# Landmark means of a Nyström attention: sums on GpSimd from q and k as they lie, in place of products on a second copy by rows

## The chip, the cores and the metric

The kernel runs on one core of a Trainium2 chip. The metric is the time of one execution on the device in microseconds; the median of the runs is what is compared. TensorE multiplies matrices, VectorE and ScalarE do elementwise work and reductions, GpSimd does elementwise work and issues the software transfers (loads), SyncE issues the stores.

## What is computed

Nyström attention over 8 batches and 8 heads, and then a feed-forward layer with a squared ReLU. The landmarks, on which the change works, are the means of 18 consecutive rows of q and of k (576 rows make 32 landmarks).

```python
q_lm = q.reshape(B, H, m, S // m, D).mean(axis=3)    # B = H = 8, S = 576, D = 64, m = 32
k_lm = k.reshape(B, H, m, S // m, D).mean(axis=3)
A = sm(q, k_lm); Bm = sm(q_lm, k_lm); C = sm(q_lm, k) # softmax of scaled products
Z = Bm.T / (norm1(Bm) * norminf(Bm) + 1e-06)          # norms over the last two axes
for _ in range(6):
    Z = 2 * Z - Z @ Bm @ Z
x = A @ Z @ C @ v                                     # then heads side by side: 4608 x 512
out = relu(x @ w_in) ** 2 @ w_out                     # 512 -> 2048 -> 512
```

All inputs and the output are fp32 in HBM.

## The kernel before

**Tiles.** A load turns q and k of one batch into bf16 in the tile X (lines 292 and 420): a partition holds one of four heads' 32 landmarks, so its row is the 18 x 64 elements that belong to one landmark; t = 0 is q and 1 is k, r is the half of the heads. Three X tiles take turns (batch b uses X of b mod 3), likewise V. A landmark is therefore a sum along a partition's own row, over 18 pieces of 64 elements.

**Landmarks.** Batches 0 to 2 sum on TensorE with an identity matrix as weights (`landmarks`, line 492). Batches 3 to 7 (`ROWS`, line 1187) load q and k a second time, by rows, into the tile XS (`load_xs`, line 427), and TensorE sums there with a 0/1 matrix `seg` as weights (`landmarks_rows`, line 477; 24 products of 256 columns a batch, line 485). VectorE or ScalarE copies the sums from PSUM with the scale 1/(8 x 18) to the bf16 tile LM (operation `lme`, lines 413 and 417); VectorE transposes them to LT (`lmt`, line 538).

**What follows on them.** From LT come the small matrix B (`B`, line 554), its softmax on VectorE and ScalarE (lines 560 to 570), the inverse by six steps, each a block-diagonal product `bd` on VectorE or GpSimd (line 630), two products on TensorE (`N`, line 693) and an update on VectorE (`U`, line 707), and the score products with q and k (`SS`, lines 724 and 729). The softmax of A takes VectorE through At, Amx, Asb, Asu and Aml (lines 1003 to 1020), that of C through Cmx (line 767) and ScalarE's Cex (line 770). The operations called `bt` (also line 630) and `BBT` begin the inverse.

**Feed-forward.** The attention is folded into the weights (`W`, line 886, copied to WP), so that the first layer is `F` (line 1050, 512 products), the ReLU `R` (line 1071 on ScalarE, 1073 on VectorE), the square `Q` (line 1078 on ScalarE, 1080 on VectorE and GpSimd) into the ring G, and the second layer `O` (line 1097, 592 products), whose result goes out through OS. The attention of a batch runs beside the feed-forward of the batches before it.

**Order.** Every operation has a name and the text ORDER (line 1204) lists them all in one sequence, with the PSUM bank (`@0`) and the engine if it isn't the first choice (`/A`, `/D`, `/P`). Each engine works through its own operations in this sequence. `Plan.schedule` (line 98) reckons with costs and due times to place filler products: `Plan.fillers` (line 160) puts products on a tile of ones (line 1171) into TensorE's gaps before the first operation O. An argument `port` marks operations of VectorE and GpSimd that the plan doesn't let overlap. GpSimd's queue holds the loads too, so a load stands behind what is ahead of it there.

Of the kernel before, what the change touches and what calls it, by code (L numbers as in the profile page):

```python
# [7 lines left out]
P = 128  # L8
# [8 lines left out]
H = 8  # L17
S = 576
D = 64
# [35 lines left out]
class Plan:  # L55
# [5 lines left out]
    BLOCK, FETCH, FETCH_LOADED, PROLOG = 256, 3.8, 6.2, 94  # L61
# [36 lines left out]
    def schedule(self, order):  # L98
# [4 lines left out]
        owner, landed, self.history, self.order = [None] * 8, [], [], []  # L103
        for word in order:
# [55 lines left out]
    def fillers(self, until, width, emit):  # L160
# [42 lines left out]
RATE = {"sw": 0.375e6, "hw": 0.2e6, "first": 0.375e6, "then": 0.405e6, "late": 0.29e6}  # L203
T0 = {"PE": 1.1, "ACT": 1.1, "DVE": 1.1, "POOL": 1.31, "SP": 1.1}
# [59 lines left out]
def kernel(  # L264
# [32 lines left out]
    XS = mk("XS", [96, 2, H, 6, D], BF16)  # L297
# [129 lines left out]
    def load_xs(b):  # L427
        for t in range(2):
            src = (q, k)[t][b].rearrange("h (p j) d -> p h (j d)", j=6)
            op(f"lx{b}.{t}", {"POOL": 0.57}, lambda e, t=t, src=src: nc.gpsimd.dma_start(  # L430
                XS[:, t].rearrange("p h j d -> p h (j d)"), src),
               W=[("XS", t)], nbytes=1179648, queue="sw")

# [25 lines left out]
    def attention(b):  # L459
# [17 lines left out]
        def landmarks_rows():  # L477
            pl_ = Bank(1, "att")
            view = lambda: bank(pl_)[:, 0:256].rearrange("p (t r d) -> p t r d", t=2, d=D)

            def lmx(e):
                xs = XS[:].rearrange("p t (r c) j d -> p t r c j d", r=2)
                for j in range(6):
                    for c in range(4):
                        nc.tensor.matmul(view()[quad(c)], lhsT=seg[:], rhs=xs[:, :, :, c, j, :],  # L485
                                         start=(j == 0), stop=(j == 5))
# [43 lines left out]
        for rs in rss:  # L530
            if b in ROWS:
                landmarks_rows()
# [600 lines left out]
    def loads(what, b):  # L1133
# [9 lines left out]
        elif what == "xs":  # L1143
            load_xs(b)
# [9 lines left out]
    for b in range(B):  # L1154
        if b in ROWS:
            loads("xs", b)
# [48 lines left out]
c0 ldk0.1 c1 ldq0.1 c13 c17 Bce0@0 ldq0.0 ldk0.0 ldq1.0 ldk1.0 c2 c14 c12 c3 lm0.1@6 ldk1.1 c5  # L1205
ldq1.1 c15 c6 c11 lmc0.10 lmc0.11 ldv0.10 ldv0.00 win10 ldv0.11 T0.11 c8 T0.01 lme0.1 lmt0.1
SC0.1@2 T0.00 T0.10 Cmx0.1 T1.00 c9 lm0.0@4 lme0.0 lmt0.0 B0@4 bk0 Bmx0 Cex0.1 CT0.1 Bsb0 Bex0
SC0.0@6 Cmx0.0 Bsu0 Brc0 win11 win01 Bml0/P SA0.1@2 Amx0.1b SA0.0@1 Amx0.0b c10 Cex0.0 Crc0 Bmb0/A
Btr0 Bcs0 Bnm0 Brn0 Amx0.0a Amx0.1a Asb0.0b Aex0.0b BBT0@4 Yi0 Asb0.1a Asb0.0a Asb0.1b Cmk0 win00
win21 Zi0/P win20 Aex0.1a lm1.0@0 lme1.0 Aex0.0a Aex0.1b N0.0@4 U0.0 N0.1@5 Asu0.0b lmt1.0 B1@0  # L1210
# [126 lines left out]
```

## Time and profile before

| | before |
|---|---|
| median of three runs, us | 264.32 |
| lowest and highest, us | 263.7 and 264.74 |
| profiled execution, us | 264.69 |
| its span, first to last instruction, us | 263.0 |
| its mean granted TensorE clock | 0.992 |

The page gives each engine's busy time over the span, then a chain of work followed back from the last instruction: shares of it tell which engine's work set the end. A row of a group reads: line, engine, operation, output and inputs, shape, count, then busy time in us, mean ns of one, and the idle time of the engine just before, with what ended it. A row of a window reads: the stretch, its length, the busy time of each engine with its instructions, the granted TensorE clock, the share of the transfer engines' time, and GB/s. A row in order of time has its start and its length in us. Line numbers are those of the kernel before.

### The profile page before, as it was taken

What the parts mean: (1) busy time and instruction counts of PE and PEld (TensorE: products, weight loads), DVE (VectorE), ACT (ScalarE), POOL (GpSimd) and SP (SyncE); (2) the same over time, 40 slices, a digit from 0 to 9 for tenths busy, and PEclk for the clock granted to TensorE, in tenths of its full rate; (3) what the DMA queues carried; (4) which work ended last, traced back from release to release, by engine and by line L of the source; (5) the groups of instructions that cost most, each with busy time, mean ns of one, the idle gap of its engine ahead of it and who ended that gap; (6) DMA issues with size and microseconds to landing.
All of it is one profiled execution on the core that took longest, in us unless ns stands there. A gap on an engine that the chain in (4) does not pass through costs nothing.

```text
span 263.0 us, 7571 instructions
## 1 busy us (share of the span) xinstructions
PE 253.5 (96%) x3098; PEld 141.0 (54%) x3098; DVE 208.8 (79%) x537; ACT 184.8 (70%) x334; POOL 75.5 (29%) x127
## 2 busy tenths in 40 slices
PE   7898999999999999999999999999999999999993
PEld 3465566466454656465545455466454655466542
DVE  2799698887999789997998999988898975657110
ACT  1552698489886799979687469797595896588211
POOL 8458675904303430140315520221010120000000
PEclk9999799999999999999999999999999999999999
DMA  6999999995997399848496399337301214053025
GB/s 105 204 185 205 209 207 205 193 208 113 196 223 151 63 205 212 204 87 176 64 231 107 46 190 227 70 60 139 96 2 40 38 31 101 2 120 81 2 61 140
DMA packets 25123, 34.18 MB, mean 130 GB/s; under 512 B 2432, under 2 KB 14464, under 8 KB 25088
## 3 DMA queue, kind: packets, MB, share of 16 engines
q0 software_dynamic: 19168, 24.25, 56.4%
q1 hardware_dynamic: 5760, 9.31, 13.1%
q8 instruction: 24, 0.39, 0.6%
q10 hardware_dynamic: 160, 0.13, 0.2%
q14 instruction: 11, 0.09, 0.1%
HBM read 48.50 MB, written 9.44 MB: 220 GB/s over the span
## 4 chain that ended last, share of the span: by engine, by line
PE 73%; DVE 15%; ACT 7%; issue 2%; POOL 2%; POOLq 0%; DVEq 0%; ACTq 0%
PE ps L1097 40%; PE ps L1050 19%; ACT RS L1071 3%; PE ps L886 3%; PE ps L815 2%; PE ps L1171 1%; DVE sm L767 1%; PE ps L729 1%; POOL X L424 1%; PE ps L485 1%; DVE G L1080 1%; ACT G L1078 1%; DVE RS L1073 1%; DVE TT L469 1%; DVE WP L415 1%
## 5 line engine op out<-in xcount | busy, mean ns | idle before, releaser
L1097 PE MATMUL ps<-w_out,G 128*128 128x512 bf16 (+1 forms) x592 | 139.1, 374 | 0.0
L1097 PEld LDWEIGHTS <-G 128*128 128x128 bf16 x592 | 54.5, 98 | 53.2 <-issue 5.5
L1050 PE MATMUL ps<-AT,WP 128*128 128x288 bf16 (+2 forms) x512 | 75.3, 286 | 0.9 <-ACT RS L1071 0.4
L1071 ACT ACTIVATE RS<-ps 128x576 bf16<-128x576 f32 (+2 forms) x99 | 62.1, 648 | 11.3 <-PE ps L1050 7.3
L1050 PEld LDWEIGHTS <-WP 128*128 128x128 bf16 x512 | 48.1, 98 | 21.9 <-issue 2.6
L1078 ACT ACTIVATE G<-RS 128x576 bf16<-128x576 bf16 (+2 forms) x80 | 53.6, 688 | 3.3 <-DVE RS L1073 2.4
L411 ACT COPY OS<-ps 128x512 f32<-128x512 f32 (+1 forms) x27 | 15.3, 568 | 18.8 <-PE ps L1097 16.2
L1073 DVE TENSOR_SCALAR RS<-ps 128x576 bf16<-128x576 f32 (+2 forms) x29 | 21.9, 757 | 7.2 <-PE ps L1050 3.5
L630 POOL TENSOR_TENSOR BD<-ST,blkb 128x256 bf16<-128x256 bf16 x15 | 10.5, 700 | 58.7 <-DVE ST L707 53.3
L411 ACT CAST WP<-ps 128x1024 bf16<-128x1024 f32 (+1 forms) x24 | 22.2, 962 | 7.2 <-PE ps L886 7.1
L469 DVE STREAM_TRANSPOSE TT<-X 128x576 uint32<-128x576 uint32 x32 | 24.0, 758 | 0.1
L1080 DVE TENSOR_TENSOR G<-RS 128x576 bf16<-128x576 bf16 (+1 forms) x40 | 18.1, 457 | 5.8 <-ACT RS L1071 5.5
L770 ACT ACTIVATE C<-ps,sm 128x576 bf16<-128x576 f32 x16 | 14.3, 906 | 11.8 <-DVE sm L767 11.8
L707 DVE SCALAR_TENSOR_TENSOR ST<-ST,ps 128x128 bf16<-128x128 bf16 (+1 forms) x48 | 12.8, 266 | 8.0 <-PE ps L693 4.7
L1171 PE MATMUL ps<-onesb 128*128 128x512 bf16 (+1 forms) x42 | 13.1, 404 | 1.5 <-DVE onesb L347 1.5
L440 POOL DMA_DIRECT2D V<-in_v_dram x24 | 13.2, 552 | 3.2 <-DMA XS<-in_k_dram 1.5
L415 DVE CAST WP<-ps 128x1024 bf16<-128x1024 f32 (+1 forms) x10 | 11.7, 1165 | 1.0 <-PE ps L886 0.9
L767 DVE TENSOR_REDUCE sm<-ps 128x1 f32<-128x576 f32 x16 | 11.6, 746 | 0.7 <-PE ps L729 0.5
L415 DVE COPY OS<-ps 128x512 f32<-128x512 f32 x10 | 6.7, 678 | 6.0 <-PE ps L1097 6.0
L630 POOL TENSOR_TENSOR BD<-Bt,blkb 128x256 bf16<-128x256 bf16 x4 | 2.7, 665 | 30.5 <-PE ps L693 17.1
L886 PE MATMUL ps<-w_in,ZC 64*32 64x512 bf16 x256 | 11.2, 397 | 0.1
L1080 POOL TENSOR_TENSOR G<-RS 128x512 bf16<-128x512 bf16 (+1 forms) x8 | 8.9, 1120 | 6.0 <-ACT RS L1071 6.0
(143 smaller groups left out, 304.3 us busy)
## 6 DMA issues: line engine op xcount, KB each, us to landing
out_dram<-OS SPq DMA_DIRECT2D x70, 128.0 KB, 2.5
X<-in_k_dram POOLq DMA_DIRECT2D x16, 288.0 KB, 9.0
X<-in_q_dram POOLq DMA_DIRECT2D x16, 288.0 KB, 7.8
XS<-in_q_dram POOLq DMA_DIRECT2D x5, 576.0 KB, 8.8
XS<-in_k_dram POOLq DMA_DIRECT2D x5, 576.0 KB, 9.9
V<-in_v_dram POOLq DMA_DIRECT2D x8, 288.0 KB, 6.1
w_in<-in_moe_w_in_dram POOLq DMA_DIRECT2D x8, 256.0 KB, 9.9
w_out<-in_moe_w_out_dram POOLq DMA_DIRECT2D x4, 512.0 KB, 9.8
```

The source lines that it names most:

```text
L411: nc.scalar.copy(o, i)
L415: eng(e).tensor_copy(o, i)
L469: op(f"T{b}.{t}{r}", {"DVE": v_(576)}, lambda e, r=r: nc.vector.transpose(tt[:, t, r].rearrange("p s m e -> p (s m e)").bitcast(U32), x[:, ...
L770: op(f"Cex{b}.{r}", {"ACT": a_(576) + 0.27}, lambda e, r=r: nc.scalar.activation(Cs[r][:].rearrange("p x u -> p u x"), cbanks(r), AF.Exp, ...
L886: nc.tensor.matmul(ps[quad(pos_a(c, r)), pW.at + r, :], lhsT=zcs[r][half, pos_c(c, r), :], rhs=w_in[half, c, 512 * ch:512 * ch + 512], sta ...
L1050: nc.tensor.matmul(ps[:, ph.at + i, 0:w], lhsT=wp[:, r, 128 * ff:128 * ff + 128], rhs=at[:, r, t0:t0 + w], start=(r == 0), stop=(r == 1))
L1071: nc.scalar.activation(rs, pair(ph, w), AF.Relu)
L1073: nc.vector.tensor_scalar(out=rs, in0=pair(ph, w), scalar1=0.0, scalar2=None, op0=ALU.max)
L1078: nc.scalar.activation(g, rs, AF.Square)
L1080: eng(e).tensor_tensor(g, rs, rs, ALU.mult)
L1097: nc.tensor.matmul(bank(po)[:, 0:c1 - c0], lhsT=G[:, f, lo:lo + P], rhs=w_out[:, f, c0:c1], start=(f == 0), stop=(f == NF - 1))
L1171: nc.tensor.matmul(ps[:, j, 0:w], lhsT=onesb[:, 0:P], rhs=x[:, 0:w], start=True, stop=True)
```

## The change

For batches 3 to 7 the tile XS, its loads and the products on it are taken out. GpSimd adds from X itself, in fp32, into the new tile SU: for each of q and k and each half of the heads the first nine pieces of 64 plus the last nine (`la`), and then for both halves together 4 + 4, 2 + 2, 1 + 1 and the ninth piece (`lb`). `lme` copies from SU instead of from PSUM. The constants of the plan are set anew, the plan's fillers take account of TensorE's stalls, and ORDER is a new sequence. The matrix `seg` is still made.

```diff
-    XS = mk("XS", [96, 2, H, 6, D], BF16)
+    SU = mk("SU", [P, 2, 2, 9, D], F32)
...
-    def load_xs(b):
-        for t in range(2):
-            src = (q, k)[t][b].rearrange("h (p j) d -> p h (j d)", j=6)
-            op(f"lx{b}.{t}", {"POOL": 0.57}, lambda e, t=t, src=src: nc.gpsimd.dma_start(
-                XS[:, t].rearrange("p h j d -> p h (j d)"), src),
-               W=[("XS", t)], nbytes=1179648, queue="sw")
...
-        def landmarks_rows():
-            pl_ = Bank(1, "att")
-            view = lambda: bank(pl_)[:, 0:256].rearrange("p (t r d) -> p t r d", t=2, d=D)
-
-            def lmx(e):
-                xs = XS[:].rearrange("p t (r c) j d -> p t r c j d", r=2)
-                for j in range(6):
-                    for c in range(4):
-                        nc.tensor.matmul(view()[quad(c)], lhsT=seg[:], rhs=xs[:, :, :, c, j, :],
-                                         start=(j == 0), stop=(j == 5))
-            op(f"lm{b}.0", {"PE": pe(256, 6) + 0.11}, lmx, R=["seg", ("XS", 0), ("XS", 1)], W=[pl_],
-               alloc=[pl_], mode="128x32", ni=48)
+        def landmarks_pool():
+            add = lambda e, o, i, y: eng(e).tensor_tensor(o, i, y, ALU.add)
+            flat = lambda a: a.rearrange("p s d -> p (s d)")
+            for t in range(2):
+                ku = [("SU", t, 0), ("SU", t, 1)]
+                for r in range(2):
+                    op(f"la{b}.{t}{r}", {"POOL": p_(576)}, lambda e, t=t, r=r: add(
+                        e, flat(SU[:, t, r]), flat(x[:, t, r, 0:9, :]), flat(x[:, t, r, 9:18, :])),
+                       R=kx(t, r), W=[ku[r]], port=("POOL",))
+                for i, (n, a, z) in enumerate(((4, 0, 4), (2, 0, 2), (1, 0, 1), (1, 0, 8))):
+                    y = SU[:, t].rearrange("p r s d -> p r (s d)")
+                    sl = lambda v, n=n: slice(D * v, D * (v + n))
+                    op(f"lb{b}.{t}{i}", {"POOL": p_(128 * n)},
+                       lambda e, y=y, sl=sl, z=z: add(e, y[:, :, sl(0)], y[:, :, sl(0)], y[:, :, sl(z)]),
+                       R=ku, W=ku, port=("POOL",))
             op(f"lme{b}.0", {"ACT": 0.1 + ap_(256), "DVE": v_(256)},
-               lambda e: copy(e, lm[:], view(), scale=LMS), R=[pl_], W=[("LM", i2, r) for r in range(2)])
+               lambda e: copy(e, lm[:], SU[:, :, :, 0, :], scale=LMS),
+               R=[("SU", t, r) for t in range(2) for r in range(2)], W=[("LM", i2, r) for r in range(2)])
...
-    BLOCK, FETCH, FETCH_LOADED, PROLOG = 256, 3.8, 6.2, 94
+    BLOCK, FETCH, FETCH_LOADED, PROLOG = 256, 3.8, 6.0, 110
...
+                    self.stalls.append((free[e], fetched))
...
-                sw += o.nbytes / RATE["first" if sw < 23.0 else "then" if sw < 48.0 else "late"]
+                sw += o.nbytes / next(r for t, r in RATES if sw < t)
...
+            at = max([at, *(y for x, y in self.stalls if at - 0.1 < x < a)])
...
+RATES = ((12.5, 0.41e6), (23.0, 0.365e6), (48.0, 0.405e6), (85.0, 0.33e6), (1e9, 0.29e6))
```

Of ORDER, which is new from its first line to its last, here is the place where batch 3's landmarks are summed, in the changed kernel:

```text
We1.2/D W1.0@2 We1.01 We1.00 O0.0@7 W1.3@4 We1.3 B2@0 Bmx2 Bsb2 Bex2 F0.24@2 R0.24 Ap1.1@0
Bsu2 Ab1.1 F0.30@4 Q0.24/A R0.30 Q0.26/A F0.14@2 R0.14/D O0.1 la3.01 la3.00 lb3.00 ldq4.1 lb3.01
ldv2.00 la3.10 F1.0@0 R1.0 Brc2 Bml2 Btf2 Bcs2 Q0.14/A Bct2 F1.2@4 F1.6@2 F0.28@0 R0.28 Q0.28/A
...
Q0.30/A F1.4@2 R1.4 la3.11 bt2 BBT2@1 lb3.10 O0.2 O2.2 F1.12@2 R1.12 O1.2 Yi2 Zi2 bd2.0/D T3.10
T2.00 lb3.02 lb3.11 lb3.03 lb3.12 ldq4.0 lb3.13 lme3.0/D N2.0@1 U2.0 F1.8@2 bd2.1/D Q1.12/A R1.8
```

By the listings of the two programs the instructions change so: 120 products on XS go (line 485); the filler products become 52 instead of 48; GpSimd issues 68 loads instead of 78, makes 60 additions of landmarks, 15 block-diagonal products instead of 19, 4 squares instead of 8, and 5 products of An (line 965) instead of 3; ScalarE and VectorE exchange single operations.

More of the change, by code (lines that the diff above doesn't have):

```diff
@@ L1223 @@
-R0.14/D Bsu2 ldk3.0 Arc1.0 Aml1.0 Q0.26/P ldv3.11 Q0.14/P ldq3.1 ldv2.11 ldq4.0 ldk3.1 Brc2 O1.1
-W1.2@2 We1.2/D W1.3@6 W1.0@4 O0.1 We1.3 We1.01 O1.2 O0.2 F0.28@6 R0.28 Ap1.0@2 Ab1.0/A Q0.28/A
-Bml2 Btf2 Bcs2 Btr2 We1.00/D bt2/D Bct2 Bnm2 Bad2 Brn2 T2.11 BBT2@3 F0.24@4 O1.3 F1.2@6 R1.2 Oe1.0
-R0.24/D Q0.24/A Q1.2/A St1 T2.01 Zi2 Yi2 T2.10 O2.0@2 F1.0@4 bd2.0/D R1.0/D F1.8@6 R1.8 O0.3
-Q1.8/A Oe0.0 N2.0@0 U2.0 bd2.1/D F1.14@4 F0.30@6 N2.1@0 U2.1 bd2.2/D R1.14 Q1.14/A R0.30/D Q0.30/A
-O2.1 F1.4@0 N2.2@3 U2.2 O2.2 bd2.3/D N2.3@3 F1.6@4 F1.12@6 O2.3 Q1.0 R1.4 R1.6 Q1.6/A Q1.4 R1.12
@@ new lines @@
+R0.12 Q0.12/A F0.26@4 ZC1@2 R0.26/D ZCe1.0 ZCe1.1 F0.8@0 R0.8 Q0.8 O2.0@6 W1.1@4 We1.1 W1.2@0
+We1.2/D Aml1.1 W1.0@2 We1.01 We1.00 O0.0@7 W1.3@4 We1.3 B2@0 Bmx2 Bsb2 Bex2 F0.24@2 R0.24 Ap1.1@0
+Bsu2 Ab1.1 F0.30@4 Q0.24/A R0.30 Q0.26/A F0.14@2 R0.14/D O0.1 la3.01 la3.00 lb3.00 ldq4.1 lb3.01
+ldv2.00 la3.10 F1.0@0 R1.0 Brc2 Bml2 Btf2 Bcs2 Q0.14/A Bct2 F1.2@4 F1.6@2 F0.28@0 R0.28 Q0.28/A
+Bnm2 Btr2/A Bad2 T3.00 R1.2/D Brn2 T2.10 T2.11 Q1.0/A R1.6 O2.1 O1.0@0 O1.1 F1.14@4 Q1.2/A Q1.6/A
+Q0.30/A F1.4@2 R1.4 la3.11 bt2 BBT2@1 lb3.10 O0.2 O2.2 F1.12@2 R1.12 O1.2 Yi2 Zi2 bd2.0/D T3.10
```

192 lines of the change are left out of this document (96 added, 96 removed).

## The prediction

> **What bounds the kernel now.** I read the page's engine table and its chain of waits first, to see which engine sets the end, then the table of windows of ten microseconds, to see where another engine does.
>
> ```profile
> span 263.0 us, 7571 instructions
> PE 253.5 (96%) x3098; PEld 141.0 (54%) x3098; DVE 208.8 (79%) x537; ACT 184.8 (70%) x334; POOL 75.5 (29%) x127
> ...
> PE 73%; DVE 15%; ACT 7%; issue 2%; POOL 2%; POOLq 0%; DVEq 0%; ACTq 0%
> PE ps L1097 40%; PE ps L1050 19%; ACT RS L1071 3%; PE ps L886 3%; PE ps L815 2%; PE ps L1171 1%; DVE sm L767 1%; PE ps L729 1%; POOL X L424 1%; PE ps L485 1%; DVE G L1080 1%; ACT G L1078 1%; DVE RS L1073 1%; DVE TT L469 1%; DVE WP L415 1%
> ```
>
> TensorE is busy for 96% of the span and carries 73% of the chain, so work taken from it is mostly time. VectorE carries 15%. The windows say where.
>
> ```profile
> core 0: us, PE busy (x) PEld busy (x) DVE busy (x) ACT busy (x) POOL busy (x), PEclk, DMA share, GB/s
> ...
> 100.00:110.00 10.00, 10.00 (x184) 5.59 (x183) 9.73 (x32) 9.30 (x17) 1.20 (x2) 1.00 1.08 235
> ...
> 150.00:160.00 10.00, 10.00 (x107) 5.50 (x106) 9.84 (x26) 6.63 (x13) 2.90 (x5) 1.00 1.14 178
> ...
> 200.00:210.00 10.00, 9.90 (x117) 5.66 (x116) 9.56 (x24) 7.93 (x15) 1.20 (x2) 1.00 0.26 44
> ...
> 40.00:175.00 135.00, 134.21 (x1753) 73.89 (x1747) 121.97 (x314) 108.16 (x192) 43.39 (x70) 1.00 0.85 154
> ```
>
> At 100, 150 and 200 us VectorE is as full as TensorE; between 40 and 175 us, where the landmarks of batches 3 to 7 are made, it has only 135.0 - 122.0 = 13.0 us idle, and GpSimd 91.6. From here on the question is what GpSimd's new work does to VectorE.
>
> **What the change removes.** The groups of instructions, with shapes kept apart, price it; the chain in order of time says how much of it counts.
>
> ```profile
> L485 PE MATMUL ps<-XS,seg 96*32 96x256 bf16 x120 | 4.2, 274 | 0.0
> L430 POOL DMA_DIRECT2D XS<-in_q_dram x5 | 4.1, 815 | 0.0
> L430 POOL DMA_DIRECT2D XS<-in_k_dram x5 | 4.1, 812 | 5.2 <-PE ps L485 5.2
> ```
> ```profile
> 63.23 0.77 PE ps L485 x24
> 87.70 0.77 PE ps L485 x24
> ...
> 99.98 0.44 DVE CT L786
> ...
> 111.44 0.36 DVE AT L1023
> ...
> 146.40 0.77 PE ps L485 x24
> ...
> 167.70 0.77 PE ps L485 x24
> ```
>
> All 120 products of line 485 go. They hold TensorE for 4.2 us, 0.84 a batch. Four of the five groups lie on the chain with 0.77 us each, 3.1 together; the fifth, of batch 5, falls between 100 and 111 us, where the chain runs along VectorE, and is worth nothing there. So the removal is worth between 3.1 and 4.2 us, and I take 3.2, near the chain. The ten loads of XS cost GpSimd 8.2 us of issue and move 10 of 78 software transfers, each twice the size of a load of X. The only transfers on the chain are the issues of the first X (line 424, 1%), so I take nothing for them. The landmark itself becomes a copy of the same 256 elements from SBUF instead of PSUM: nothing either, since it stays one instruction on VectorE or ScalarE.
>
> **What it adds.** Sixty additions on GpSimd, twelve a batch: four of 576 elements (bf16 in, fp32 out), then for q and for k one each of 512, 256, 128 and 128 in fp32. No GpSimd addition from bf16 to fp32 is in this trace; the nearest rows bound it.
>
> ```profile
> L1080 POOL TENSOR_TENSOR G<-RS 128x512 bf16<-128x512 bf16 x7 | 7.7, 1100 | 6.0 <-ACT RS L1071 6.0
> L965 POOL TENSOR_TENSOR An<-SA,smA 128x320 bf16<-128x320 f32 x2 | 1.5, 739 | 0.0
> L570 POOL TENSOR_TENSOR Bf<-Bl,sm 128x64 f32<-128x64 f32 x3 | 0.9, 293 | 16.6 <-ACT RS L1071 8.2 <-DVE sm L617 6.6 <-DVE sm L568 1.7
> ```
>
> The two fp32 rows give (739 - 293) / (320 - 64) = 1.74 ns an element and 0.18 us fixed. That makes 1.18 us for 576, 1.07 for 512, 0.63 for 256, 0.40 for 128: per batch 4 x 1.18 + 2 x (1.07 + 0.63 + 0.80) = 9.7 us, and 48.6 for five. The bf16 row (1.10 for 512) agrees to 3%. Upper end: the 512-element row with its steps scaled, 1.24 for 576, 51 us in all. GpSimd goes from 43.4 to 43.4 - 8.2 + 48.6 = 84 us in a window of 135: it fits. By itself this costs nothing; what covers it is GpSimd's own 91.6 us of idle time. The path from landed q and k to the landmark becomes 9.7 us instead of 0.77, but the order written down issues a batch's loads of X a batch or more ahead.
>
> The price is VectorE. It and GpSimd disturb each other:
>
> ```profile
> L1080 DVE TENSOR_TENSOR G<-RS 128x576 bf16<-128x576 bf16 x38 | 17.3, 459 | 5.3 <-ACT RS L1071 5.1
> ...
> L630 POOL TENSOR_TENSOR BD<-ST,blkb 128x256 bf16<-128x256 bf16 x15 | 10.5, 700 | 58.7 <-DVE ST L707 53.3 <-DVE ST L654 5.5
> ...
> L630 POOL TENSOR_TENSOR BD<-Bt,blkb 128x256 bf16<-128x256 bf16 x4 | 2.7, 665 | 30.5 <-PE ps L693 17.1 <-PE ps L1050 10.3 <-issue 3.1
> ```
> ```profile
> 106.02 0.66 POOL L630 TENSOR_TENSOR BD<-Bt,blkb 128x256 bf16<-128x256 bf16 x1 [10.32 <-PE ps L1050]
> 106.23 0.77 DVE L1080 TENSOR_TENSOR G<-RS 128x576 bf16<-128x576 bf16 x1
> 106.92 0.81 DVE L1014 TENSOR_REDUCE smA<-SA 128x20 f32<-128x640 f32 x1
> ...
> 194.31 0.64 DVE L1080 TENSOR_TENSOR G<-RS 128x576 bf16<-128x576 bf16 x1
> ```
>
> A square on VectorE takes 0.459 us on average, but 0.77 when it starts inside a GpSimd product that ends at 106.68, and 0.64 at 194.31. It lost 0.31 and 0.18 us. Lower end: these 0.49 us fell beside 10.5 + 2.7 = 13.2 us of such products, so 48.6 us of additions cost VectorE 48.6 / 13.2 x 0.49 = 1.8 us, and 15% of that, VectorE's share of the chain, is 0.3 us. The upper end counts every VectorE instruction with two inputs in SBUF:
>
> ```profile
> L630 DVE TENSOR_TENSOR BD<-ST,blkb 128x256 bf16<-128x256 bf16 x21 | 5.9, 283 | 0.4
> L1020 DVE TENSOR_TENSOR An<-SA,smA 128x640 bf16<-128x640 f32 x6 | 5.3, 892 | 0.1
> L849 DVE TENSOR_TENSOR ZM<-ST,blk 64x128 bf16<-64x128 bf16 x24 | 5.1, 213 | 0.5
> L1010 DVE TENSOR_TENSOR SA<-SA,smA 128x640 f32<-128x640 f32 x6 | 4.9, 818 | 0.1
> ...
> L1020 DVE TENSOR_TENSOR An<-SA,smA 128x512 bf16<-128x512 f32 x6 | 4.3, 724 | 0.1
> L1010 DVE TENSOR_TENSOR SA<-SA,smA 128x512 f32<-128x512 f32 x6 | 4.1, 680 | 0.0
> ```
>
> With the 38 squares these are 107 instructions. One meets an addition with chance 48.6 / 135 = 0.36 and then waits half a mean addition, 0.81 / 2 = 0.4 us: 107 x 0.36 x 0.4 = 15.4 us of VectorE, and at 15% 2.3 us. I take 1.2, midway, because the additions are longer and follow each other more closely than the products of line 630.
>
> The Trainium skill (SBUF — State Buffer, section Who interferes with whom) has a rule that speaks against this change: a VectorE instruction with two SBUF inputs and a GpSimd instruction that reads SBUF exclude each other, and whoever issues second blocks fully. The 0.77 us at 106.23 agrees. By the rule alone the term would be the upper end, and the first rival below is what it does when VectorE's idle time runs out.
>
> **What it moves.** The whole order is new. By the programs' listings VectorE gains 3 ReLUs, 2 squares, 2 copies of AT and 4 block-diagonal products and gives away 2 of the three An products of line 965, a cast of WP, an output copy, 4 copies of ZC and 2 scalings of C; ScalarE gets the copies and scalings and 2 squares more and loses 3 ReLUs. At the rows' prices neither changes by more than some 4 us, beside 263.0 - 208.8 = 54 us idle on VectorE and 78 on ScalarE: nothing. On GpSimd's queue, loads and products now stand behind additions that wait for loads: behind batch 3's additions on k stand the block-diagonal product bt2, for which BBT2 and the whole inverse of batch 2 wait, and the loads of q 4 and v 2. That is a rival, not a term.
>
> The start changes too. It holds the only throttled stretch before the end:
>
> ```profile
> 24.00:26.00 2.00, 1.12 (x18) 0.60 (x17) 1.83 (x6) 0.16 (x1) 1.74 (x4) 1.00 1.24 204
> 26.00:28.00 2.00, 1.94 (x20) 1.56 (x21) 1.91 (x7) 0.85 (x2) 1.50 (x3) 0.61 1.14 206
> 28.00:30.00 2.00, 2.00 (x37) 0.64 (x37) 0.99 (x3) 1.05 (x2) 1.64 (x3) 0.54 1.20 217
> ```
>
> After 2 us in which TensorE was busy for 1.12, the granted clock falls to one half: means of 0.61 and 0.54 over 2 us each are (0.39 + 0.46) x 2 / 0.5 = 3.4 us at half speed. With TensorE full in them that cost up to 1.7 us. The new order has 52 filler products on ones instead of 48 and counts none inside a stall of instruction fetch. Ends: -1.7 if the stretch goes, +1.7 if a second comes. I take -0.8, half way to gone.
>
> **Sum.** Against the profiled execution (span 263.0, its own time 264.69, so 1.69 around it): -3.2 + 1.2 - 0.8 = -2.8, a time of 261.9. The three runs' median, 264.32, lies 0.37 below that execution, so the forecast for the median is 261.5.
>
> **Rivals.** *VectorE becomes the bound (slower).* The mechanism is the exclusion above, at the place where VectorE is full, 100 to 110 and 150 to 160 us. With 15.4 us of waits it needs 122.0 + 15.4 = 137.4 us in the window of 135: 2.4 more than before, and TensorE's gain is lost. The time is 264.3 + 2.4 = 266.7. It decides once VectorE waits over 13 us in all. For it: three windows at 96% and more. Against it: the two seen waits total 0.49 us. 23%.
>
> *The landmarks come late (about as before).* Additions wait for loads and bt2 waits behind them; if each of five batches loses 0.5 us so, 2.5 of the 2.8 us go: 264.0. For it: loads of X take 8 to 9 us to land. Against it: the same loads, without those of XS, find more room. 10%.
>
> *The gain is hidden anyway (no change).* TensorE's 3.1 us on the chain turn up as waits in the stretches that VectorE sets: 264.3. For it: those three windows. Against it: 73% of the chain. 9%.
>
> That the products or loads are still there is excluded: the listing of the new program has none. Only the making of the matrix seg is left over, 0.4 us on GpSimd beside loads.
>
> **How the numbers follow.** The forecast has 58%; its own range is 261.5 with the ends of its terms, 258.8 to 263.0. The range over all cases is 258.8 to 266.0; the upper end leaves out the worse half of the slow rival and the lower some 6%. A difference under 0.5%, that is 263.0 to 265.6, can't be told from no change here: the second and third rivals, 19%. Faster 58%, slower 23%.
>
> **What would show it.** Right: line 485 gone; GpSimd some 40 us busier, additions of 576 at 1.1 to 1.3 us; squares on VectorE mostly at 0.46 with some of 0.8 to 1.6; TensorE some 4 us less busy and still at 95% or more; the granted clock at one half at most once before the end. Wrong: VectorE at 97% and more from 60 to 170 us with squares averaging over 0.6 us, TensorE's idle time ended by VectorE, or ST and LM waited for through GpSimd.

## The result, and the profile after

The changed kernel takes 273.4 us (272.1 to 274.16, four runs) beside 264.02 us for the kernel before on the same chip: a ratio of 1.035, with an interval from 1.030 to 1.039. The profiled execution took 273.62 us, with a span of 271.9. The forecast was 261.5 us. The page's engine table and its chain read:

```profile
span 271.9 us, 7371 instructions
PE 252.9 (93%) x2982; PEld 138.9 (51%) x2982; DVE 225.1 (83%) x534; ACT 186.1 (68%) x341; POOL 119.5 (44%) x173
...
PE 49%; DVE 35%; ACT 5%; issue 3%; DVEq 0%; ACTq 0%
```

TensorE's share of the chain has gone from 73% to 49%, VectorE's from 15% to 35%, and VectorE is busy for 225.1 us in place of 208.8. The products of line 485 are gone, and GpSimd is 44.0 us busier. Where the time was lost shows in the windows, of before first and then of after:

```profile
core 0: us, PE busy (x) PEld busy (x) DVE busy (x) ACT busy (x) POOL busy (x), PEclk, DMA share, GB/s
45.00:75.00 30.00, 30.00 (x318) 15.98 (x316) 26.27 (x68) 23.33 (x41) 12.47 (x18) 1.00 1.04 183
75.00:105.00 30.00, 29.91 (x462) 16.71 (x461) 26.82 (x76) 25.73 (x47) 7.80 (x13) 1.00 0.93 166
```
```profile
45.00:75.00 30.00, 27.19 (x280) 14.62 (x265) 27.15 (x61) 21.82 (x39) 25.27 (x33) 1.00 0.96 182
75.00:105.00 30.00, 24.02 (x296) 11.41 (x295) 28.68 (x60) 23.01 (x40) 18.47 (x24) 0.94 0.51 89
105.00:175.00 70.00, 69.17 (x833) 38.54 (x832) 65.58 (x168) 56.90 (x100) 32.22 (x45) 1.00 0.45 90
...
82.00:84.00 2.00, 2.00 (x22) 0.61 (x29) 1.90 (x6) 0.00 (x0) 0.67 (x2) 0.50 1.10 207
```

From 45 to 105 us TensorE now has 2.8 + 6.0 = 8.8 us without work where it had 0.1. VectorE did fewer instructions there (121 for 144) and was busy for longer. After 105 us TensorE is full again, though GpSimd is still adding. The granted clock of 0.94 from 75 to 105 us is one stretch at half clock, 3.4 us from 81.3 us, behind 4 us (78 to 82) in which TensorE was busy for 1.3; the one execution without a loss of clock (mean 1.000) took 272.1 us, the other three (0.991 to 0.994) 273.2 to 274.2.

The list of TensorE's waits names who ended them (instruction, releaser, us in all, times, longest):

```profile
PE ps L1098 <- DVE ST L708: 2.6, 2, 2.2
PE ps L694 <- DVE BD L631: 2.3, 2, 1.5
PE ps L555 <- DVE LT L539: 1.6, 2, 1.0
PE ps L1168 <- DVE onesb L351: 1.5, 1, 1.5
PE ps L641 <- DVE BD L631: 1.2, 1, 1.2
PE ps L699 <- DVE ST L708: 1.1, 1, 1.1
```

All of these are VectorE's products, none GpSimd's (line 1168 is at the start, 1.5 us as before). The groups with shapes kept apart price GpSimd's additions and show which VectorE instructions grew:

```profile
L475 POOL TENSOR_TENSOR SU<-X 128x576 f32<-128x576 bf16 x20 | 26.1, 1316 | 12.9 <-ACT LM L417 5.3 <-DVE ZM L850 4.0 <-DVE LM L421 3.6
L475 POOL TENSOR_TENSOR SU<-SU 128x512 f32<-128x512 f32 x10 | 13.9, 1396 | 0.3
L475 POOL TENSOR_TENSOR SU<-SU 128x256 f32<-128x256 f32 x10 | 8.4, 839 | 0.3
L475 POOL TENSOR_TENSOR SU<-SU 128x128 f32<-128x128 f32 x20 | 9.2, 466 | 0.6
```
```profile
L1081 DVE TENSOR_TENSOR G<-RS 128x576 bf16<-128x576 bf16 x38 | 17.2, 458 | 6.3 <-ACT RS L1072 5.9
L631 DVE TENSOR_TENSOR BD<-ST,blkb 128x256 bf16<-128x256 bf16 x24 | 9.8, 408 | 0.4
L421 DVE TENSOR_SCALAR C<-C,sm 128x576 bf16<-128x576 bf16 x8 | 4.5, 573 | 0.0
L571 DVE TENSOR_TENSOR Bf<-Bl,sm 128x64 f32<-128x64 f32 x4 | 3.5, 885 | 0.0
```

The additions took 57.6 us, not 48.6. The squares of line 1081 kept their 0.46 us; the block-diagonal products BD went from 0.283 to 0.408 us, and the product Bf of 64 elements from 0.201 us before to 0.885, a mean of four of which one stood for 2.45. The rows in order of time show how (start, length):

```profile
51.30 0.58 POOL L437 DMA_DIRECT2D V<-in_v_dram  x1
51.88 0.15 DVE L569 RECIPROCAL sm<-sm 128x2 f32<-128x2 f32 x1
51.90 2.52 POOL L475 TENSOR_TENSOR SU<-X 128x576 f32<-128x576 bf16 x2
52.06 2.45 DVE L571 TENSOR_TENSOR Bf<-Bl,sm 128x64 f32<-128x64 f32 x1
...
96.87 1.30 POOL L475 TENSOR_TENSOR SU<-X 128x576 f32<-128x576 bf16 x1
96.98 1.75 DVE L1011 TENSOR_TENSOR SA<-SA,smA 128x512 f32<-128x512 f32 x1
98.25 3.63 POOL L475 TENSOR_TENSOR SU<-SU 128x512 f32<-128x512 f32 x3
98.65 1.35 DVE L631 TENSOR_TENSOR BD<-ST,blkb 128x256 bf16<-128x256 bf16 x1
99.92 1.38 DVE L421 TENSOR_SCALAR C<-C,sm 128x576 bf16<-128x576 bf16 x1
101.22 1.34 DVE L1011 TENSOR_TENSOR SA<-SA,smA 128x640 f32<-128x640 f32 x1
```

Bf came 0.16 us after a pair of additions had begun and ended 0.09 us after both were over. At 97 us four instructions in a row each stood until the addition beside it had ended: 5.8 us for what cost 0.68 + 0.28 + 0.36 + 0.82 = 2.1 by the means of before (0.361 for the scaling C). Below, the excess of a VectorE instruction is its length beyond the median of its group before, where it is over 0.1 us. It sums to 1.7 us before and 19.6 after.

### The profile page after: what moved, and what is told of

Same layout as the page of the kernel before. It is cut to its first block, busy times and chain, and to the rows that moved or that the text cites. A ratio compares the mean times of both kernels' runs of the same rounds, so it can differ in the third digit from the quotient of the medians.

```text
span 271.9 us, 7371 instructions
## 1 busy us (share of the span) xinstructions
PE 252.9 (93%) x2982; PEld 138.9 (51%) x2982; DVE 225.1 (83%) x534; ACT 186.1 (68%) x341; POOL 119.5 (44%) x173
## 4 chain that ended last, share of the span: by engine, by line
PE 49%; DVE 35%; ACT 5%; issue 3%; DVEq 0%; ACTq 0%
PE ps L1098 28%; PE ps L1051 14%; DVE RS L1074 3%; DVE SA L1011 3%; DVE An L1021 3%; DVE G L1081 2%; DVE BD L631 2%; DVE WP L419 2%; DVE SA L1004 2%; DVE ZM L850 2%; PE ps L887 2%; ACT G L1079 2%; DVE sm L768 2%; DVE ST L708 2%; ACT RS L1072 1%
## 5 line engine op out<-in xcount | busy, mean ns | idle before, releaser
L1072 ACT ACTIVATE RS<-ps 128x576 bf16<-128x576 f32 (+2 forms) x96 | 60.4, 652 | 16.5 <-PE ps L1051 7.1
L1079 ACT ACTIVATE G<-RS 128x576 bf16<-128x576 bf16 (+2 forms) x82 | 54.8, 683 | 7.6 <-DVE RS L1074 6.8
L475 POOL TENSOR_TENSOR SU<-X 128x576 f32<-128x576 bf16 x20 | 26.1, 1316 | 12.9 <-ACT LM L417 5.3
L475 POOL TENSOR_TENSOR SU<-SU 128x128 f32<-128x128 f32 (+2 forms) x40 | 31.2, 792 | 1.2
L631 POOL TENSOR_TENSOR BD<-ST,blkb 128x256 bf16<-128x256 bf16 x12 | 9.3, 779 | 43.9 <-DVE ST L708 24.4
L1074 DVE TENSOR_SCALAR RS<-ps 128x576 bf16<-128x576 f32 (+2 forms) x32 | 23.6, 741 | 3.0 <-PE ps L1051 1.9
L1081 DVE TENSOR_TENSOR G<-RS 128x576 bf16<-128x576 bf16 (+2 forms) x42 | 20.2, 484 | 6.9 <-ACT RS L1072 6.6
L1004 DVE STREAM_TRANSPOSE SA<-ps 128x320 f32<-128x320 f32 (+1 forms) x24 | 10.0, 456 | 1.7 <-PE ps L725 1.6
L1011 DVE TENSOR_TENSOR SA<-SA,smA 128x640 f32<-128x640 f32 (+1 forms) x12 | 11.3, 943 | 0.0
```

The source lines that it names most:

```text
L475: add = lambda e, o, i, y: eng(e).tensor_tensor(o, i, y, ALU.add)
L1011: lambda e, sa=sa, bA=bA: eng(e).tensor_tensor(fl(sa), fl(sa), bA(0), ALU.subtract),
L1072: nc.scalar.activation(rs, pair(ph, w), AF.Relu)
L1074: nc.vector.tensor_scalar(out=rs, in0=pair(ph, w), scalar1=0.0, scalar2=None, op0=ALU.max)
L1079: nc.scalar.activation(g, rs, AF.Square)
L1081: eng(e).tensor_tensor(g, rs, rs, ALU.mult)
```

## The experiments

**Order or additions?** The first run shortens the additions; the second adds some to the kernel before.

```diff
-  e, flat(SU[:, t, r]), flat(x[:, t, r, 0:9, :]), flat(x[:, t, r, 9:18, :])),
+  e, SU[:, t, r, 0, :], x[:, t, r, 0, :], x[:, t, r, 9, :]),
...
-  add(e, y[:, :, sl(0)], y[:, :, sl(0)], y[:, :, sl(z)]),
+  add(e, SU[:, t, 0, 0, :], SU[:, t, 0, 0, :], SU[:, t, 1, 0, :]),
```


> The changed kernel with its order, its 60 additions and all their dependences, but each addition works on 64 elements only, so most of the landmark sum is left out. An addition of 64 fp32 elements took about 0.29 us in the trace of before, so GpSimd's additions shrink from 57.3 us to some 18. Theory (long GpSimd additions hold off VectorE's instructions with two SBUF inputs, and those waits reach the end): the waits go and the gain of the removed products shows, 258 to 262 us. Rival A (the new order is worse by itself, whatever GpSimd does): 270 us or more, as the changed kernel's 273.4. Rival B (it is GpSimd's queue that is late, loads and the block-diagonal product standing behind additions): 258 to 262 us as well; this run does not tell it from the theory.

Measured: 261.41 us, ratio 0.989 (0.985 to 0.993), excess 3.9 us, TensorE 250.0 us busy and 76% of the chain. The order is sound: the length of the additions costs 273.4 - 261.4 = 12.0 us. The loss of clock is in it, since the short additions ran at 0.999 to 1.000; beside the changed kernel's execution at 1.000 it is 10.7.

```diff
+    for i in range(28):
+        op(f"exa{i}", {"POOL": p_(512)}, lambda e: nc.gpsimd.tensor_tensor(
+            bkf, w_in[:, 0, 0:512], w_in[:, 0, 512:1024], ALU.add), R=kw, W=["BK"], port=("POOL",))
+        op(f"exb{i}", {"POOL": p_(256)}, lambda e: nc.gpsimd.tensor_tensor(
+            cp, w_in[:, 0, 1024:1280], w_in[:, 0, 1280:1536], ALU.add), R=kw, W=["cpick"], port=("POOL",))
```


> The kernel before, with its order, loads and products untouched, and 56 extra GpSimd additions (28 of 512 elements from bf16 to bf16, 28 of 256 from bf16 to fp32) between 50 and 176 us, put where GpSimd was idle; nothing reads what they write and they wait for nothing but weights that landed long before. Some 48 us of GpSimd work is added and nothing else. Theory (exclusion): VectorE's instructions with two SBUF inputs wait 10 to 18 us in all and the time rises by 5 to 10 us, to 269 to 275. Rival A (the order): 264 to 265, since this is before's order. Rival B (GpSimd's queue): up to 266, since the additions stand in gaps.

Measured: 286.3 us, ratio 1.084 (1.079 to 1.089), far above the 5 to 10 us more that were expected. The excess is 26.3 us, 24.6 more than before, and the time rose by 22.4. Nothing waits for these additions, and of TensorE's waits GpSimd ended 0.9 us (0.3 before); what the additions do to VectorE is the price, in this order too. One place of it in order of time:

```profile
126.58 0.58 POOL L424 DMA_DIRECT2D X<-in_k_dram  x1 [1.03 <-DVE sm L617]
126.97 3.76 DVE L621 TENSOR_SCALAR sm<-sm 128x2 f32<-128x2 f32 x1
127.18 1.17 POOL L1170 TENSOR_TENSOR BK<-w_in 128x512 bf16<-128x512 bf16 x1
128.30 0.67 POOL L1172 TENSOR_TENSOR cpick<-w_in 128x256 f32<-128x256 bf16 x1
128.93 1.14 POOL L1170 TENSOR_TENSOR BK<-w_in 128x512 bf16<-128x512 bf16 x1
130.04 0.66 POOL L1172 TENSOR_TENSOR cpick<-w_in 128x256 f32<-128x256 bf16 x1
```

An instruction on two elements stood for 3.76 us, through four additions that have nothing to do with it.

**The wait by itself.** 

> A small program that measures the exclusion by itself; it computes none of the reference. Sections, one after the other: eight squares of 576 bf16 elements on VectorE beside a train of eight independent GpSimd additions of 576 elements; the same beside a chain of eight additions each of which needs the one before; then one-input tensor_scalar and tensor_reduce beside the train; squares beside memsets of 128 to 4608 fp32 elements and beside DMA issues. Theory: beside the train of independent additions a square starts and then stands still until the whole train is over (10.5 us for eight additions of 1.3), beside the dependent chain each square waits for at most about one addition (0.9 to 1.4 us); memsets and DMA issues delay a square by under 0.1 us. Rival (each addition only slows a square by half an addition, as the prediction had it): 0.46 + 0.4 = 0.9 us on average in both sections.

The squares, tensor_scalars and reductions beside GpSimd's work, in order of time (x8 is eight in a row):

```profile
26.92 10.57 DVE L42 TENSOR_TENSOR G<-RS 128x576 bf16<-128x576 bf16 x8
27.04 11.57 POOL L39 TENSOR_TENSOR SU<-X 128x576 f32<-128x576 bf16 x8
...
53.14 4.24 DVE L104 TENSOR_SCALAR G<-G,sm 128x576 bf16<-128x576 bf16 x4
53.26 10.15 POOL L39 TENSOR_TENSOR SU<-X 128x576 f32<-128x576 bf16 x8
...
64.38 5.90 DVE L110 TENSOR_REDUCE sm<-SA 128x1 f32<-128x640 f32 x8
64.50 9.86 POOL L39 TENSOR_TENSOR SU<-X 128x576 f32<-128x576 bf16 x8
...
75.33 3.06 DVE L42 TENSOR_TENSOR G<-RS 128x576 bf16<-128x576 bf16 x8
75.43 8.34 POOL L116 MEMSET SU<- 128x128 f32 x6
```

Eight squares took 10.57 us beside additions and 3.06 us beside memsets: 1.32 for 0.38 each. Neither theory had it: squares and additions take turns, so that each square costs one addition, in the chain as well (eight in 11.33 us). One-input tensor_scalars pay too, 1.06 us each, where three alone took 0.92 in all; reductions do not (0.74 each, as alone). Memsets and the issue of loads cost the squares nothing. The Trainium skill (SBUF — State Buffer, section Who interferes with whom) has these same lines: two SBUF inputs or a 2-port mode contend, a reduction does not, and for two inputs a GpSimd instruction that only writes doesn't matter. Here the trace agrees for the squares, the reductions and the memsets; which mode the tensor_scalars ran in no run shows.

**Queue or exclusion, and where.**

```diff
-  e, flat(SU[:, t, r]), flat(x[:, t, r, 0:9, :]), flat(x[:, t, r, 9:18, :])),
+  nc.gpsimd.memset(every[:, min(576 * (2 * t + r), 844):min(576 * (2 * t + r), 844) + FILL(576)], 0.001 + t + r),
```


> The changed kernel with its order, each of the 60 additions replaced by a GpSimd memset of about the same duration (1460, 1556, 887 and 439 fp32 elements; memsets took 0.83 us per 1000 elements plus 0.1 in the small program, so 1.32, 1.40, 0.84 and 0.46 us, the means of the additions). GpSimd's queue is as full as in the changed kernel, but nothing reads SBUF; the landmark sum is left out, and the memsets wait for no load. In the small program squares took 0.38 us each beside memsets, as without them. Theory (exclusion of instructions, not time on the queue): about 260 to 262.5 us, as with the short additions (261.4) or a little less, and VectorE's excess under 3 us. Rival (the queue: loads, block-diagonal products and landmarks stand behind 57 us of work): 268 to 274.

Measured: 263.12 us, ratio 0.996 (0.994 to 0.999), with 58.3 us of memsets. Holding GpSimd's queue for that long costs at most 1.7 us; the other 10.3 of the 12.0 come with the reading of SBUF, or with waits for loads, which the memsets do not have. The profile with memsets also has a stretch at half clock, from 26.7 us, ahead of the first row of the table below, where it is already 1.00 us late. The excess missed its expectation: 10.3 us, in part because instructions behind a held one are counted with it. What was held were above all tensor_scalars (a sum sm of two elements 1.02 us beside a memset); little of it reached the end.

```diff
+  e, SU[:, t, r, 0, :], x[:, t, r, 0, :], x[:, t, r, 9, :]) if b < 6 else add(
   e, flat(SU[:, t, r]), flat(x[:, t, r, 0:9, :]), flat(x[:, t, r, 9:18, :])),
```


> The changed kernel with full additions in batches 6 and 7 only; those of batches 3, 4 and 5 work on 64 elements each, so most of their landmark sums is left out. In the trace of the changed kernel the matrix products fall behind between 47 and 105 us, where the additions of batches 3 to 5 run (45.8 to 113.2 us), and not after. Theory (the price is local: it is paid where the inverse of batch 2 and the first softmaxes leave TensorE nothing else to do): 261 to 263 us, within 1.5 us of the kernel with all additions short (261.4). Rival (every addition costs alike): 24 of 60 additions full, 261.4 + 0.4 x 12.0 = 266.2 us.

Measured: 263.31 us, ratio 0.998 (0.996 to 0.999). The 24 additions of batches 6 and 7 cost 1.9 us, the 36 of batches 3 to 5 cost 10.1. All these kernels issue the same 2982 weight loads to TensorE in the same order, so the start of the n-th can be compared. The table gives how late it is, in us, beside the run with short additions (left, its time there); the last two columns are runs told further on.

```text
short   after  memset  full 6,7  chain  gaps
 47.2   -0.38    1.00     -0.25  -0.29  -0.64
 59.4    1.70    1.11     -0.26   5.34   1.24
 75.7    3.87    1.12     -0.26   5.95   1.63
 88.0    6.30    1.17     -0.26   6.60   1.89
104.3   10.17    2.35     -0.27   7.49   3.09
120.7   10.37    2.33     -0.10  12.91   3.27
161.7   11.69    2.31      1.30  13.39   5.45
251.9   11.61    2.31      1.27  13.30   5.45
```

The changed kernel loses 10.2 of its 11.6 us before 105 us, and what is lost is not won back. In its profiled execution the stretch at half clock is in this, up to 1.7 us.

**Why some instructions stand so long.** 

> A second small program; it computes none of the reference. VectorE alternates a reduction (which was not held off in the first) with one short instruction, beside a train of GpSimd additions, so that the short instruction comes while an addition is under way, as it does in the kernels. Sections: squares; tensor_scalar of two fp32 elements; products of 64 fp32 elements; the tensor_scalar beside additions of 512 and 256 in turn; squares beside loads with additions right behind them; squares beside one-input GpSimd instructions. Theory 1 (VectorE gets its turn at the next end of an addition): no instruction lasts longer than one addition plus its own time, 1.8 us for a square, 1.5 for the others. Theory 2 (an instruction that comes in mid-addition can lose its turn, as in the extra-additions kernel, where a tensor_scalar of two elements stood for 3.76 us through four additions): some last 2.4 us or more. Beside loads alone: under 0.6 us.

Squares that came while an addition was under way lasted 0.79 to 0.87 us, tensor_scalars and small products 0.56 to 1.09: theory 1, except in one section. There a square at 61.58 us, just behind four loads, stood for 5.15 us through all four additions. Beside one-input GpSimd instructions squares lasted 0.92 to 0.96 us.

> A third small program; it computes none of the reference. In the second, a square that came while the first of four additions right behind four loads was under way stood for 5.15 us through all four, though without loads ahead squares got in at each end of an addition. Sections, VectorE alternating reductions with squares in all: one load, then four independent additions; one load, then four additions in a chain; one load, two tiny dependent additions, then four; three times a load and an addition; one load, then twelve additions of 128; the same twelve without a load; one load and four additions beside tensor_scalars of two elements. Theory (a load right ahead makes the additions behind it one closed stretch): squares of over 3 us in the first and fifth section and a tensor_scalar of over 2.4 us in the last, none over 1.9 us in the second and sixth. Rival (chance of arrival): long ones in any section, or in none.

The first and the third section, in order of time:

```profile
13.04 0.70 POOL L77 DMA_DIRECT2D Y<-in_q_dram  x1
...
13.76 4.95 POOL L41 TENSOR_TENSOR SU<-X 128x576 f32<-128x576 bf16 x4
13.78 5.25 DVE L44 TENSOR_TENSOR G<-RS 128x576 bf16<-128x576 bf16 x1
...
32.20 0.27 POOL L103 TENSOR_TENSOR pq<-RS 128x2 f32<-128x2 f32 x1
...
32.55 0.19 POOL L104 TENSOR_TENSOR pq<-pq,RS 128x2 f32<-128x2 f32 x1
32.70 5.60 POOL L41 TENSOR_TENSOR SU<-X 128x576 f32<-128x576 bf16 x4
33.08 1.21 DVE L44 TENSOR_TENSOR G<-RS 128x576 bf16<-128x576 bf16 x1
```

Behind a load the four additions were one closed stretch, 5.25 us for a square and 5.20 for a tensor_scalar of two elements. Behind a load, an addition, a load and an addition, a square stood for 3.95 us. Two small additions with a dependence between them opened the stretch (1.21 us); so did a chain (1.85 us, then 0.92). The fifth section missed its expectation: its squares lasted at most 0.71 us behind a load, but the first of them had begun before the first addition.

**Short pieces without and with gaps.** The sum in four pieces of 144 and so on, all independent:

```diff
+  [add(e, flat(SU[:, t, r])[:, c:c + 144], flat(x[:, t, r, 0:9, :])[:, c:c + 144],
+       flat(x[:, t, r, 9:18, :])[:, c:c + 144]) for c in range(0, 576, 144)],
```


> The changed kernel with the same sums, but in short pieces: each addition of 576 elements as four of 144, each of 512 as four of 128, each of 256 as two of 128; nothing is left out. An addition of 128 took 0.466 us and four independent ones follow each other, so GpSimd's additions grow from 57.3 us to 20 x 4 x 0.48 + 10 x 4 x 0.46 + 10 x 2 x 0.46 + 20 x 0.46 = some 75 us, while one piece is a third as long. Theory (VectorE's short instructions wait for the end of the addition under way, so the price goes with the length of one addition): VectorE's excess falls from 19.6 to about 8 us and the time to 266 to 269. Rival (the price goes with GpSimd's total time beside VectorE, or VectorE loses its turn for whole trains whatever the pieces are): 274 to 278.

Measured: 278.31 us, ratio 1.055 (1.050 to 1.061), excess 23.8 us; the theory fell. A BD at 102.31 us stood for 4.67 us through ten pieces, with no load right ahead. Short additions are no help while they follow each other closely.

```diff
+  add(e, gap[:], SU[:, t, r, 8, 0:2], SU[:, t, r, 8, 2:4])],
```


> The changed kernel with one addition of two elements behind each of the 20 additions of 576, which reads what that addition wrote and so cannot start before it has ended; nothing is left out. In the third small program such a dependence ended the closed stretch behind a load: a square then waited for one addition, not for four. Theory (VectorE loses whole trains of additions behind loads, and those waits lie on the path): in the trace of the changed kernel four VectorE instructions stood through more than one addition or through loads (46.62, 52.06, 62.37 and 77.84 us), some 4 us together; most of it returns, 269 to 271 us, though the small additions cost GpSimd 5 us. Rival (waits for single additions make the price): 273 to 275.

Measured: 272.02 us, ratio 1.029 (1.025 to 1.032): between the two expectations, excess 18.6 us. Bf still stood for 2.86 us, through load, addition, load, addition; the gap was in the wrong place.

```diff
+  [add(e, flat(SU[:, t, r, 0:3, :]),
+       flat(SU[:, t, r, 0:3, :]) if c else flat(x[:, t, r, 0:3, :]),
+       flat(x[:, t, r, 3 + 3 * c:6 + 3 * c, :])) for c in range(5)],
```


> The changed kernel with the same sums in another grouping: each addition of 576 becomes a chain of five of 192 elements, each of which adds three segments to the running sum of three and needs the one before, and two additions of 128 for each of q and k close it; nothing is left out. GpSimd's additions take about 100 x 0.52 + 20 x 0.46 = 61 us, more than the changed kernel's 57.3 and less than the 72.6 of the independent short pieces (278.3 us). Theory (VectorE gets in at each gap that a dependence leaves, and waits at most for one short addition): no VectorE instruction loses over 0.6 us to the sums, the excess is 5 to 9 us, and the time 263 to 267. Rival (what counts is how long GpSimd adds in all): 273 to 278.

Measured: 275.14 us, ratio 1.039 (1.033 to 1.044), with the excess down to 9.2 us. The waits shrank as the theory said, and the time did not. TensorE's waits in this kernel say why:

```profile
PE ps L644 <- POOL BD L634: 3.9, 1, 3.9
PE ps L697 <- POOL BD L634: 3.9, 1, 3.9
```

Now GpSimd ended them: with 69.2 us of sums in its queue, bt2 and bd4.2 stood behind two chains each. In the table the chain loses 5.6 us up to 59 us, 5.4 before 121, and 2.6 elsewhere.

**The two products off the queue.**

```diff
-la3.11 bt2 BBT2@1
+la3.11 bt2/D BBT2@1
...
-N4.1@2 U4.1 bd4.2
+N4.1@2 U4.1 bd4.2/D
```


> The chain of short additions (275.1 us) with two block-diagonal products moved from GpSimd to VectorE, bt2 and bd4.2; nothing else changes and nothing is left out. In that kernel's trace TensorE fell behind in two places only by more than 1 us: 5.5 us before the product that needs bt2 (59.5 us, queued on GpSimd behind 20 pieces) and 5.4 us before the one that needs bd4.2 (127.9 us). Theory (the chain has cured VectorE's waits, and what is left is the two products' place in GpSimd's queue): 263.5 to 266. Rival (VectorE's remaining 9 us of excess or another late landmark takes their place): 268 to 272.

Measured: 271.84 us, ratio 1.029 (1.026 to 1.032). Of these 11.0 us, 3.3 came back: bt2 was cured, but behind bd4.2 another product of GpSimd took its place (TensorE waited 3.3 us for it, and 1.6 for ST of GpSimd).

The next two share an order in which four products of GpSimd go to VectorE and some loads and pieces of sums stand elsewhere (core of it):

```diff
-la3.11 bt2 BBT2@1
+la3.11 bt2/D BBT2@1
...
-Bml3/P
+Bml3
...
-Zi3/P
+Zi3
...
-bd4.2
+F3.4@4 bd4.2/D
```


> The chain of short additions with bt2, bd4.2, Bml3 and Zi3 on VectorE, and four loads, six landmark pieces and copies and three other words of the order shifted by a few places so that less stands behind the chains; nothing is left out. Theory: VectorE's waits stay short (excess 6 to 10 us, none over 0.6 us beside a sum) and GpSimd's queue is late nowhere by more than 1 us, so the time is that of the short additions (261.4) plus 1 to 2.5 us: 262 to 264, below the kernel before (264.0). Rival: 265 to 268, some new product late behind a chain.

> The same order as the kernel before this one in the list, but with the changed kernel's own additions (576, 512, 256, 128) in place of the chains. Theory (long independent additions hold VectorE off, whatever stands behind them on GpSimd): 267 to 272. Rival (in the changed kernel, too, it was bt2 and bd4.2 behind the additions that cost the time): 262 to 265.

Measured: 267.56 us (266.94 to 269.22; ratio 1.013, 1.010 to 1.016) with chains and 272.48 us (ratio 1.034, 1.028 to 1.040) with the long additions in the same order. The rival of the second is out: with bt2 and bd4.2 on VectorE the long additions cost as much as ever. The first missed its 262 to 264; excess 9.9 us.

**Opening the stretches.**

```diff
+  add(e, gap[:, 2:4], x[:, t, r, 0, 0:2], x[:, t, r, 0, 2:4]),
+  add(e, gap[:, 4:6], gap[:, 2:4], gap[:, 2:4]),
   add(e, flat(SU[:, t, r]), flat(x[:, t, r, 0:9, :]), flat(x[:, t, r, 9:18, :])),
+  add(e, gap[:, 0:2], SU[:, t, r, 8, 0:2], SU[:, t, r, 8, 2:4])],
```


> The changed kernel with three additions of two elements around each of the 20 additions of 576: two ahead of it, the second of which needs the first, and one behind, which needs it; nothing is left out. In the third small program two such additions between a load and a train opened the stretch (squares of 1.21 and 0.79 us in place of 5.25). With a gap behind the additions alone the product Bf still stood for 2.86 us (51.29 to 54.15 us), through load, addition, load, addition. Theory: no VectorE instruction stands longer than one addition, 1.4 us above its own time, the Bf of that place under 1.7 us, and the time is 269 to 271.5 us, since the waits for single additions of 1.3 us remain; so closed stretches made 2 to 4 us of the loss. Rival (closed stretches made most of it): below 267.

Measured: 267.58 us, ratio 1.0125 (1.0084 to 1.0166). The additions are as long as before and there are 60 small ones more, yet 5.8 of the 12.0 us are back. The largest excess is 1.04 us (2.24 in the changed kernel), the sum 12.0. No execution here lost clock (0.997 to 1.000); beside the changed kernel's execution at 1.000, 272.1 us, 4.5 us are back. Part of it may be chance of arrival: Bf now ran at 51.00 us, ahead of the load that had closed the stretch. So open stretches were worth 4.5 to 5.8 us, where 2 to 4 were expected.

```diff
+  add(e, flat(SU[:, t, r, 0:6, :]), flat(x[:, t, r, 0:6, :]), flat(x[:, t, r, 6:12, :])),
+  add(e, flat(SU[:, t, r, 0:6, :]), flat(SU[:, t, r, 0:6, :]), flat(x[:, t, r, 12:18, :])),
...
-la3.11 bt2 BBT2@1
+la3.11 bt2/D BBT2@1
```


> The kernel with three small additions around each long one (267.6 us), with two changes: each addition of 576 becomes two of 384, the second needing the first, and the block-diagonal product bt2 goes to VectorE, since TensorE waited 1.0 us for it through GpSimd; the closing additions are then one of 384 and two of 128 for each of q and k, and nothing is left out. Theory (what is left is waits for single additions, in proportion to their length, and products behind additions): single additions of 0.9 in place of 1.3 us take a third of VectorE's remaining 10 us of excess, and bt2 gives 1 us: 264.5 to 266.5 us. Rival (the small additions and the longer queue eat it): 267 to 269.

Measured: 269.03 us, ratio 1.017 (1.015 to 1.020). The rival: the excess fell to 9.2 us, but with 74.6 us of sums products stood behind them on GpSimd again (1.7 us for BD and 1.5 for ST in TensorE's waits). No version that computes the whole sum on GpSimd came below the kernel before.

## Why the prediction was wrong

*The removal and the start: not contradicted, and not shown apart.* The forecast took 3.2 + 0.8 us off. With the additions cut short the kernel gains 2.6 us, while VectorE's excess is 2.2 us above before's. The stretch at half clock belongs to single executions, not to the order: of the seven executions of before beside the short additions three had a mean clock of 0.991 to 0.993 and took 264.8 to 265.2 us, the other four, at 0.998 to 1.000, 263.7 to 263.9. With the new order it lies at 26.7 us in the profile with memsets, at 81.3 us in that of the changed kernel, and nowhere before the end in that with short additions. So the 0.8 us were read off one execution of before, and the two terms were not run apart.

*The range was narrower than its terms.* Added up, the ends of the three terms give 264.3 - 5.6 = 258.7 and 264.3 + 0.9 = 265.2 us; the upper end of 263.0 is the border of what could be told from no change. The measured 273.4 lies outside both.

*The additions' own length: 16% low.* 48.6 us were forecast and 57.6 measured; the fp32 additions of 512 took 1.40 us in place of 1.07. "By itself this costs nothing" held nearly: the memsets cost 1.7 us at most.

*The step that failed is the VectorE term,* "I take 1.2, midway", from 1.8 to 15.4 us of waits at 15%. It was wrong three times over.

1. The waits were 19.6 - 1.7 = 17.9 us, beyond the upper end. A wait was taken to be half of one addition, 0.4 us. In the small programs only a square that came alone in mid-addition lost that little (0.79 to 0.87 us for 0.44); one behind the other, each lost nearly a whole addition, and in a closed stretch one stood for 5.25 us. And the count of 107 left out one-input instructions, the scalings C and the sums sm, which stood as well.
2. Two thirds or more reached the end, not 15%: beside the run with short additions the excess is 15.7 us higher and the time 12.0 (10.7 without a loss of clock); the extra additions put 24.6 us on the excess of before and 22.4 on its time. The 15% is VectorE's share of a chain over the whole span, in a kernel where it hardly waited. Between 45 and 105 us the chain that set the end now runs largely along VectorE's instructions, many of them small (Bf, the sums sm, BD), while TensorE had 8.8 us without work. What the additions run beside decides. Of the 19.6 us of excess 12.6 lie between 45 and 105 us, beside 31 of the 60 additions; beside the other 29, up to 200 us, it is 4.2, and TensorE had 0.8 us without work. The late stretch is not safe by itself: with the extra additions in the order of before it held 16.1 us of excess, and TensorE was without work for 13.8. And beside the memsets an excess of 10.3 us cost 1.7.
3. "Midway" had no reason in the rows: the additions were known to follow each other more closely than the products that gave the lower end. That end counted two squares, 0.49 us of the 1.7 us of excess in before; one product there had lost more than both, 0.69 us, beside a square of GpSimd:

```profile
47.76 1.26 POOL L1080 TENSOR_TENSOR G<-RS 128x640 bf16<-128x640 bf16 x1
...
48.69 1.42 DVE L965 TENSOR_TENSOR An<-SA,smA 128x512 bf16<-128x512 f32 x1
```

*The rival on the slow side had the mechanism and not the price.* Its point of decision, 13 us of waits, was passed with 17.9. It priced only the overflow of a window of 135 us, 2.4 us, as if a wait at one place could be made up at another. The table shows that it was not: the losses of 45 to 105 us stay to the end. It named 100 to 110 and 150 to 160 us; the second lost nothing. The Trainium skill's rule, SBUF — State Buffer, section Who interferes with whom, was quoted as the upper end. Its sentence "Whoever issues first gets the shared pair for the whole instruction", which stands there with the 2-port modes, fits the squares that take turns with additions (1.32 us each); a square that stood through four additions (5.25 us) goes beyond one instruction, and there the measurement decides.

*Late landmarks, 10%.* In the changed kernel TensorE waited 0.2 us for GpSimd, beside 0.3 before. The mechanism is real all the same: with the chain of short additions TensorE fell 11.0 us behind at two products, though moving both gave only 3.3 us back.

*The signs.* TensorE's idle time ended by VectorE was a sign named, and it came. Squares over 0.6 us and VectorE at 97% were named too and did not come: the waits fell on BD, Bf, SA and C, and VectorE was at 91% and 96% in the two windows of loss. The squares alone do not show the loss.

What stays open: of the 6.2 us that were left with open stretches, how much are waits for single additions and how much is GpSimd's longer queue. In the order with four products moved and chains of short additions TensorE waited 0.2 us for GpSimd; its excess is 6.0 us and its time 6.1 us above the run with short additions, so there waits for single additions could be all of it. That is argued from the sums, not shown apart.

## What to carry to other kernels

Before work is given to an idle GpSimd, look for the VectorE instructions that it will run beside, above all small ones that TensorE waits for; price each that meets an addition at up to a whole addition, and at more where additions follow each other. Where TensorE has nothing else to do, count most of it: here two thirds to nine tenths. If GpSimd must add there, leave a dependence between additions, above all behind loads, and see what else stands in its queue. A share of the chain is a price only for work that keeps its place.

## What the runs showed of the hardware

- VectorE's short instructions can stand through a whole run of GpSimd instructions, loads among them: 5.25 us through four additions, 3.95 us through addition, load, addition, load, 4.67 us through ten pieces. A gap from a dependence (some 0.07 us between the additions of a chain) ended it in both sections tried; in the kernel a gap behind each long addition alone did not (Bf 2.86 us). What closes a stretch that has no load right ahead was not found.
- A tensor_scalar on two fp32 elements is held as long as a square of 576: 5.20 us behind a load, and it costs 0.15 us alone.
- The split of each sum of 576 into four independent additions of 144, and of those of 512 and 256 into pieces of 128, made the kernel 4.9 us slower, not faster. Its profiled execution has two stretches at half clock, the changed kernel's one.
- The granted clock was at one half for 3.4 us behind 2 us with TensorE busy for 1.12 (before, from 26.4 us) and behind 4 us with 1.3 (changed kernel, from 81.3 us). In the run with short additions 2 us with 1.14 (26 to 28 us) were followed by none, and executions of one kernel differ in it.
